# Attention and a two-layer MLP on one core: the last pair of chunks as seven block products, one more staging slot, four sums moved to VectorE, and ranks in the static order

## The chip, the cores and the metric

The kernel runs on one core of one Trainium2 chip. The metric is the device time of one execution in microseconds (us), as the median of several executions of each kernel. Lines named L... are lines of the kernel before.

## The reference

For 4 batches, 12 heads, 448 tokens and a head size of 64, all in float32:

```python
scores = scale * q @ k.T                    # per head, 448 x 448
scores = cap * tanh(scores / cap)           # cap = 30
attn = exp(scores) / sum(exp(scores))
x = attn @ v                                # heads joined: 4 x 448 x 768
u = x + (x.T @ U @ V).T                     # U: 448 x 32, V: 32 x 448
out = u + relu(u @ w_ch1) @ w_ch2           # 768 -> 3072 -> 768
```

## The kernel before

The program is written as a list of tasks. Each task names the engine (or engines) it may run on, a duration in a planner's units, what it reads and writes, and a priority; a smaller number goes first. A list scheduler (`Plan.simulate`) runs the tasks on a model of the five engines, and the order in which it starts them is the order in which each engine's instructions are then written down. Buffers are given out in that run as well: a buffer waits until a slot of one of its pools is free. The chip sees only the fixed order of each engine and the waits between them. SyncE (SP) issues the loads and the stores, GpSimd (POOL) issues the DMAs that add onto a tile or that rearrange, ScalarE (ACT) keeps weights in DRAM.

Attention comes first. The 24 pairs of heads are taken four at a time (`four`). For each block of keys TensorE makes scores (L459), ScalarE takes tanh (L464) and exp (L474), TensorE multiplies by v (L488 for the last 64 keys of two pairs, L500 for three blocks of 128 keys), and VectorE adds up the exponentials of the three blocks (`add`, L506, into tile es). `normalize` then handles two pairs: TensorE sums es over the partitions by a matmul with ones (L539, tile misc), the sums go to sr, POOL spreads them over the partitions (r<-sr), VectorE takes reciprocals, POOL writes them to DRAM and broadcasts them back (rb<-rd, L563), and VectorE multiplies (`norm`, L568, u<-u,rb). For the last 64 keys there are two ways. Pairs 0 to 11 (p < ALONE = 12) add them into es on VectorE by a third L506 on 64 partitions; pairs 12 to 23 leave them to four more matmuls on TensorE per `normalize` (L542, `rest`). `mixin` makes the products with U and V (L590 transposes, L606, L626) and adds onto u (L630).

The MLP follows in two halves of two batches each (n = 0 and 1), 12 chunks of 256 hidden rows in each half. The up products of a chunk are seven block products of nine matmuls instead of eight (`up_seven`, L829); the operands x are made by `operands` and the weights ws by `strassen_weights` (L657, L664). Weights of the first half are loaded from the inputs (wr<-in_w, 768 KB) and kept in DRAM in converted form, the second half loads the kept ones. In the first half each chunk is multiplied down by plain products (`down`, L894, six matmuls a group). In the second half the chunks of a pair are multiplied down together as seven block products (`down_seven`, L1021, operands in `down_operands`), with 126 matmuls for a pair. QUADS = 5 says that five of the six pairs go this way; the last two chunks go by `down`, with 144 matmuls.

A result that has to be added onto u takes one of two ways: VectorE adds it (L899, L1039), or ScalarE copies it to a staging tile st and POOL issues a DMA that adds it (a pour: L907, L1044). The tiles cx of `up_seven` in the first half and st share one set of slots of 128 x 448, five in all: two in pool xe and three that lie in space that attention leaves. A slot is free when its pour has landed. Last, `last_sums` (L1050) adds the three blocks of tile vs (shown as g) onto both halves of the last batch on VectorE.

Of the kernel before, what the change touches and what calls it, by code (L numbers as in the profile page):

```python
# [19 lines left out]
DM = H * D  # L20
# [16 lines left out]
ALONE = 12  # L37
FILL, FIRST = 18, 5
# [3 lines left out]
class Pool:  # L42
# [19 lines left out]
    def part(self, b, opened):  # L62
        if self.whole is None:
            p, g = self.within
            self.whole = opened(p).tile([128, NP, S], self.parts[0], tag=g, name=self.name, bufs=1)
        return self.parts[1][self.at(b)][b.slot](self.whole)
# [194 lines left out]
class Build(Plan):  # L261
    def __init__(self, tc, qk, v, u, vv, w1, w2, cap, ident, out):
# [8 lines left out]
        self.wp = Pool("wp", {"wa": 2, "w1": 3, "g": 3, "ws": 4, "ta": 3}, shared={"gp": "g"})  # L271
        self.wx = Pool("wx", {"x": 1})
        self.wq = Pool("wq", {"wr": 2}, shared={"wl": "wr"})
        self.pre = Pool("pre", {"th": 3, "qk": 2, "es": 2})
        self.xe = Pool("xe", {"x": 3, "cx": 2}, after=(self.pre,), shared={"st": "cx"})
# [4 lines left out]
        self.gx = [Pool("gx", {"g": 1}, after=(self.an, self.aq), within=w, shared={"gp": "g"}) for w in ((self.aq, "xx"), (self.an, "rb"))]  # L280
        self.ap = Pool("ap", {"qk": 3, "vn": 2, "th": 4, "es": 2}, side="right")
        self.late = Pool("late", {"x": 4, "ws": 3, "wa": 1}, after=(self.ap,), side="right")
# [109 lines left out]
    def attention(self):  # L392
# [8 lines left out]
        self.gz = Pool("gz", {"gp": 3}, after=(self.g0,), within=(self.ua, "u0"), parts=(F32R, {"gp": thirds}))  # L401
# [15 lines left out]
    def four(self, p):  # L417
# [26 lines left out]
        for g in range(7):  # L444
# [3 lines left out]
            for j in range(2):  # L448
# [22 lines left out]
                self.task({"ACT": 920}, tanh, r=[(ps, 0)], w=[(th, j)], prio=prio)  # L471
# [7 lines left out]
        for h in range(2):  # L479
# [12 lines left out]
            for i, o in enumerate(os):  # L492
# [31 lines left out]
    def normalize(self, p):  # L524
# [5 lines left out]
        rest = p >= ALONE  # L530
# [105 lines left out]
    def operands(self, bs, order, prio):  # L636
# [3 lines left out]
        pools = (self.wx, self.xe, self.late) if bs[0] == 0 else (self.xe, self.late)  # L640
# [71 lines left out]
    def weights(self, f, first, begin, prio):  # L712
        tag, pool = ("w1", self.wp) if first or f // CF != 2 * QUADS else ("wl", self.wq)
        w = self.buf(tag, [128, 2, DM], F32R, pool)
# [19 lines left out]
    def moe(self):  # L734


        self.kept, rest = {}, []
        order, pend = 10, None
        for n, bs in enumerate(((0, 1), (2, 3))):
# [6 lines left out]
            for c in range(NCH):  # L746
# [3 lines left out]
                four = n and c < 2 * QUADS  # L750
# [12 lines left out]
                if four and c % 2 == 0:  # L763
                    pools = (self.gw, self.g1)
                    if c < 2 * QUADS - 2:
                        pools = (self.g0, *pools) if c % 4 else (*pools, self.g0)
                    last = {(b, j): self.buf("gq", [128, 2, S], F32, *pools) for b, j in ((1, 1), (0, 0), (0, 1), (1, 0))}
                for k, _ in zip(turns, self.up_seven(bs, fs, xs, ws, gs, order, last if four else None, c % 2)):
# [5 lines left out]
                if four:  # L774
                    if c % 2:
                        gq = last
                elif n:
                    rest.append((bs, fs, w1, gs, False))
                    if c == NCH - 1:
                        for _, fs, w1, _, _ in rest:  # L780
                            w1.update((f, self.weights(f, False, 0, 3)) for f in fs)
                else:
                    pend = bs, fs, w1, gs, True
                order += 20
        self.last_sums(bs, vs)
        for x in rest:
            for _ in self.down(order, *x):
                pass
            order += 20

    def relu(self, b, f, src, key, gs):
        nc = self.nc
        tag, pools = ("g", (self.wp, *self.gx)) if b < 2 else ("gp", (self.gz, self.wp, *self.gx))
        g = gs[b, f] = self.buf(tag, [128, 2, S], F32R, *pools)
# [8 lines left out]
    def up_seven(self, bs, fs, xs, ws, gs, order, gq, k):  # L803
# [5 lines left out]
        for x in ("c22", "c11", "c12"):  # L809
            cx[x] = gq[blocks[x]] if gq else self.buf("cx", [128, S], F32, self.xe, *self.rows)  # L810
# [70 lines left out]
    def down(self, order, bs, fs, w1, g, pour):  # L881
        nc = self.nc
        for i, b in enumerate(bs):
            u = self.u_bufs[b]
            for d in range(ND):
# [17 lines left out]
                if pour and k % 2:  # L903
                    st = self.buf("st", [128, S], F32, self.xe, *self.rows)
# [9 lines left out]
                if fs[-1] == NF - 1:  # L914
                    self.task({"SP": 350}, lambda b=b, d=d, u=u: nc.sync.dma_start(
                        out=self.out[b, 128 * d:128 * d + 128], in_=u.t[:, d]), r=[(u, d)], lat=2500, prio=-200)
# [3 lines left out]
    def down_operands(self, m, gq, prio):  # L920
# [9 lines left out]
        H = DM // 2  # L930

# [27 lines left out]
        def w_slot(p):  # L959
            w = wo[p] = self.buf("w1", [128, 2, 2, H], F32R, self.wp)  # L960
            return [((lambda i=i: w.t[:, i]), [(w, i, k) for k in range(2)]) for i in range(2)]

        def g_slots(p):
            h, l = go[p] = [self.buf("g", [128, 2, S], F32R, self.wp, *self.gx) for _ in range(2)]
# [4 lines left out]
        for p in PORDER:  # L969
# [30 lines left out]
    def down_seven(self, order, bs, m, gq, vs):  # L1000
        nc = self.nc
        wo, go = self.down_operands(m, gq, 3)
# [4 lines left out]
        at = iter([o + 3 * i + 1 + e for h, o in enumerate((order, order + 20)) for i in range(7) for e in range(1 + (i + h) % 2)])  # L1007
        bank = {}
        for n, (p, d) in enumerate((p, d) for p in PORDER for d in range(3)):
# [24 lines left out]
            yield  # L1034

    def onto(self, ps, out, key, pour):
# [5 lines left out]
        st = self.buf("st", [128, S], F32, self.xe, *self.rows)  # L1042
# [4 lines left out]
    def last_sums(self, bs, vs):  # L1047
        for u, d0 in ((self.u_bufs[bs[1]], 0), (self.u_bufs[bs[1]], 3)):
            for d in range(3):
                self.task({"DVE": 620}, lambda u=u, d=d, d0=d0: self.nc.vector.tensor_tensor(  # L1050
# [57 lines left out]
```

## Time and profile before

| what | us |
|---|---|
| median of 3 executions | 870.61 |
| lowest and highest | 863.97, 870.93 |
| profiled execution, its own time | 869.8 |
| span of the profiled execution | 867.9 |

The span runs from the first to the last instruction of the program; 1.9 us of the execution lie around it. TensorE is the engine PE; its weight loads are the row PEld. Granted clock 1.00 is 2.4 GHz, and a stretch with a smaller mean holds time at 1.2 GHz. "idle before" is the time that an engine stood before an instruction, with what ended it.

### The profile page before, as it was taken

To read this page: it belongs to the slowest core of one execution; us is meant where nothing else is said; L and a number is where in the kernel's file an instruction comes from. 1 tells how busy PE (TensorE), PEld (TensorE's weight loads), DVE (VectorE), ACT (ScalarE), POOL (GpSimd) and SP (SyncE) were. 2 spreads that over 40 slices of the span, in tenths; PEclk is the share of its full clock that TensorE was granted. 3 is DMA by queue.
4 is the path that set the end of the run, shared out by engine and by line. 5 is a ranking of instruction groups with operands and counts; after the bars stand their busy time and mean duration, and the time that the engine had idled before them with its cause. 6 is when DMAs were issued, how large, how long until landed. Compare 5 with 4: busy or idle time off the path is not lost.

```text
span 867.9 us, 11802 instructions
## 1 busy us (share of the span) xinstructions
PE 851.3 (98%) x4314; PEld 677.4 (78%) x4314; DVE 678.5 (78%) x1131; ACT 518.2 (60%) x771; POOL 134.2 (15%) x174
## 2 busy tenths in 40 slices
PE   9999998999999999998999999999999999999998
PEld 5343442435899999997999999999999999999997
DVE  2798887867987777876777789788888788888864
ACT  7999897987554555535554455455655555555610
POOL 0111111111121111211111111101111111211110
PEclk9999999999999999999999999999999999999999
DMA  6753344422578787897887754914426354452413
GB/s 220 251 166 102 119 140 133 129 65 60 147 212 263 207 248 204 221 244 215 220 249 203 231 161 92 269 40 98 133 43 163 77 137 96 78 164 42 98 33 128
DMA packets 49338, 132.38 MB, mean 153 GB/s; under 512 B 6496, under 2 KB 25344, under 8 KB 49280
## 3 DMA queue, kind: packets, MB, share of 16 engines
q1 hardware_dynamic: 23024, 79.29, 28.3%
q0 software_dynamic: 19344, 33.46, 21.3%
q10 hardware_dynamic: 6912, 18.88, 5.5%
q8 instruction: 34, 0.56, 0.3%
q14 instruction: 24, 0.20, 0.1%
HBM read 79.28 MB, written 24.47 MB: 120 GB/s over the span
## 4 chain that ended last, share of the span: by engine, by line
PE 53%; DVE 0%; issue 0%
PE mm L829 25%; PE mm L1021 15%; PE mm L894 13%; DVE cx L842 0%; DVE u L899 0%; DVE wa L308 0%
## 5 line engine op out<-in xcount | busy, mean ns | idle before, releaser
L829 PE MATMUL mm<-x,ws 128*128 128x448 f32 x1512 | 333.6, 367 | 1.2 <-DVE x L664 1.2
L829 PEld LDWEIGHTS mm<-x,ws 128*128 128x128 f32 x1512 | 283.7, 188 | 27.4 <-DVE x L664 1.5
L894 PE MATMUL mm<-g,w 128*128 128x448 f32 x864 | 188.1, 367 | 2.5 <-ACT st L254 2.0
L894 PEld LDWEIGHTS mm<-g,w 128*128 128x128 f32 x864 | 162.8, 189 | 17.3 <-ACT st L254 2.4
L1021 PE MATMUL mm<-g,w 128*128 128x448 f32 x630 | 139.9, 366 | 0.0
L254 ACT ACTIVATE st<-mm 128x448 f32<-128x448 f32 x121 | 65.9, 545 | 120.1 <-PE mm L894 61.8
L1021 PEld LDWEIGHTS mm<-g,w 128*128 128x128 f32 x630 | 118.2, 188 | 10.6
L907 POOL DMA_DIRECT2D u<-st x72 | 62.9, 873 | 265.1 <-ACT st L254 265.1
L464 ACT ACTIVATE th<-sc,qsc 128x896 f32<-128x896 f32 x84 | 80.5, 1005 | 11.2 <-PE sc L459 7.0
L899 DVE TENSOR_TENSOR u<-u,mm 128x448 f32<-128x448 f32 x96 | 59.4, 620 | 34.1 <-PE mm L894 32.3
L459 PE MATMUL sc<-qk 64*128 64x448 f32 (+1 forms) x384 | 76.8, 567 | 1.2 <-ACT th L464 1.2
L474 ACT ACTIVATE th<-th,capt 128x1792 f32<-128x1792 f32 x42 | 75.3, 1794 | 1.0
L1044 POOL DMA_DIRECT2D u<-st x45 | 38.8, 863 | 218.8 <-ACT st L254 173.8
L500 PE MATMUL o<-th,vn 128*64 128x448 f32 x288 | 59.4, 548 | 0.0
L664 DVE TENSOR_TENSOR ws<-ta,ws 128x384 fp32r<-128x384 f32 x96 | 52.9, 552 | 7.0 <-ACT ws L254 6.6
L308 DVE SCALAR_TENSOR_TENSOR wa<-wa,wr 128x768 int32<-128x768 int32 (+2 forms) x50 | 46.7, 936 | 14.1 <-ACT wa L300 13.2
L459 PEld LDWEIGHTS sc<-qk 64*128 64x128 f32 (+1 forms) x384 | 26.8, 173 | 34.4 <-issue 18.8
L506 DVE TENSOR_TENSOR es<-es,th 128x896 f32<-128x896 f32 (+1 forms) x36 | 39.1, 1087 | 11.6 <-ACT th L474 11.1
L300 ACT ACTIVATE wa<-wr 128x768 f32<-128x768 f32 (+2 forms) x50 | 44.0, 884 | 3.9 <-DMA kept<-wa 1.8
L254 ACT ACTIVATE cx<-mm 128x448 f32<-128x448 f32 x42 | 22.9, 545 | 38.0 <-PE mm L829 24.6
L500 PEld LDWEIGHTS o<-th,vn 128*64 128x64 f32 x288 | 18.5, 136 | 34.5 <-issue 32.4
L1039 DVE TENSOR_TENSOR u<-u,mm 128x448 f32<-128x448 f32 x45 | 27.9, 620 | 22.3 <-PE mm L1021 20.9
(116 smaller groups left out, 984.4 us busy)
## 6 DMA issues: line engine op xcount, KB each, us to landing
wr<-in_w SPq DMA_DIRECT2D x48, 768.0 KB, 5.8
u<-st POOLq DMA_DIRECT2D x117, 224.0 KB, 4.1
kept<-wa ACTq DMA_DIRECT2D x48, 384.0 KB, 5.9
qk<-in_qk SPq DMA_DIRECT2D x24, 448.0 KB, 4.1
wa<-kept SPq DMA_DIRECT2D x28, 384.0 KB, 4.0
wr<-kept SPq DMA_DIRECT2D x20, 384.0 KB, 4.0
vn<-in_v SPq DMA_DIRECT2D x12, 448.0 KB, 3.9
rb<-rd POOLq DMA_DIRECT2D x24, 224.0 KB, 3.9
```

The lines of the kernel that those rows point to most:

```text
L254: e.activation(out=out, in_=in_, func=func)
L308: nc.vector.scalar_tensor_tensor(out=a_t().bitcast(I32), in0=a_t().bitcast(I32), scalar=3, in1=raw_t()[:, 0::2], op0=ALU.logical_shift_lef ...
L459: nc.tensor.matmul(ps.t[out, a, :S], qks[c].t[hd, 1, 128 * t:min(S, 128 * t + 128)], qks[c].t[hd, 0], start=True, stop=True)
L464: nc.scalar.activation(out=th.t[:, j], in_=ps.t[:, :, :S], func=AF.Tanh, scale=self.qsc)
L474: nc.scalar.activation(out=th.t, in_=th.t, func=AF.Exp, scale=self.capt)
L500: nc.tensor.matmul(o.t[64 * a:64 * a + 64, :S], vn.t[:, 3 * i + t, a], th.t[:, j, a], start=False, stop=t == 2)
L664: e.tensor_tensor(out=lo, in0=src(), in1=hi.bitcast(F32), op=ALU.subtract)
L829: nc.tensor.matmul(ps.t[:, :S], ws[p].t[:, wi, sl], xs[p].t[:, xi, d], start=fresh and n == 0, stop=n == 8, skip_group_check=not fresh)
L894: nc.tensor.matmul(ps.t[:, :S], w1[f].t[:, wi, sl], g[b, f].t[:, gi], start=f == fs[0] and i == 0, stop=f == fs[-1] and i == 2)
L899: nc.vector.tensor_tensor(out=u.t[:, d], in0=u.t[:, d], in1=ps.t[:, :S], op=ALU.add)
L907: nc.gpsimd.dma_start(out=u.t[:, d], in_=st.t, accum_op=ALU.add)
L1021: nc.tensor.matmul(ps.t[:, :S], w[:, wi, k, sl], g[gi][:, k], start=fresh and n == 0, stop=n == 5, skip_group_check=not fresh)
```

## The change

- The sixth pair of chunks of the second half also goes through `down_seven` (QUADS is gone). It takes its products in another order, PLAST = 3, 1, 6, 5, 2, 7, 4, and four more places for operands (pools `fin`) in space that the x tiles leave. Of its results the first five products pour (product 5 excepted, which VectorE adds straight onto both halves of the last batch), the last two are added by VectorE. The stores of the second half stand behind it.
- `last_sums` becomes two POOL DMAs that add three blocks (672 KB) each.
- One more slot for cx and st, in pool wp; the scratch of POOL's DMA descriptors goes from 4096 to 2048 bytes a partition.
- SUMS = 20 takes the place of ALONE for the sums: pairs 12 to 19 add their last 64 keys on VectorE, and only pairs 20 to 23 keep the matmuls.
- `rank` adds a fixed number to the priorities of attention's stages and of the preparation for the MLP, and multiplies some planned DMA delays. EARLY, the order in which the first half's operands are made, is another.

```diff
-QUADS = 5
+PAIRS = NCH // 2
 PORDER = 2, 3, 1, 6, 5, 7, 4
+PLAST = 3, 1, 6, 5, 2, 7, 4
-EARLY = 5, 6, 3, 2, 7, 1, 4
+EARLY = 5, 6, 2, 3, 4, 1, 7
 ALONE = 12
+SUMS = 20
+RANK = (
...
+    ("four.add", 47),
...
+    ("normalize.sums", -175),
...
+    ("convert", 108),
...
+)
-        self.wp = Pool("wp", {"wa": 2, "w1": 3, "g": 3, "ws": 4, "ta": 3}, shared={"gp": "g"})
+        self.wp = Pool("wp", {"wa": 2, "w1": 3, "g": 3, "ws": 4, "ta": 3, "cx": 1}, shared={"st": "cx"})
...
+        self.fin = [Pool("fin", {"w1": 1, "g": 1}, after=(p,), within=(p, "x"), parts=(F32R, {
+            "w1": [w1], "g": [lambda t: t[:, 4:6]]})) for p in (self.xa, self.xa, self.xl, self.xl)]
...
-                if p < ALONE:
+                if p < SUMS:
...
-        rest = p >= ALONE
+        rest = p >= SUMS
...
         self.last_sums(bs, vs)
-        for x in rest:
-            for _ in self.down(order, *x):
-                pass
-            order += 20
+        for _ in self.down_seven(order + 10, bs, PAIRS - 1, gq, vs):
+            pass
...
+            elif p == 5 and final:
+                for x in (d, 3 + d):
+                    self.onto(ps, *block(u1, x), False)
             else:
-                self.onto(ps, out, key, n % 2)
+                self.onto(ps, out, key, n % 2 if not final else n < 15)
...
     def last_sums(self, bs, vs):
...
+        u = self.u_bufs[bs[1]]
+        for d0 in (0, 3):
+            self.task({"POOL": 1000}, lambda d0=d0: self.nc.gpsimd.dma_start(
+                out=u.t[:, d0:d0 + 3], in_=vs.t, accum_op=ALU.add), r=[(vs, d) for d in range(3)],
+                w=[(u, d0 + d) for d in range(3)], lat=9000, prio=-200)
+
+    def rank(self):
+        for t in self.tasks:
...
+            if -150 < t.prio < 0:
+                t.prio += next((r for x, r in RANK if stage.startswith(x)), 0)
+            if t.lat:
+                t.lat *= next((k for x, k in SLOW.items() if stage.startswith(x)), 1)
```

The ranks and the larger SUMS move instructions on every engine. Three places matter below.

SP, the loads in the middle and at the end of attention (in_qk and in_v are attention's, in_w the MLP's weights of 768 KB). Before:

```order
L433 DMA qk<-in_qk 128x896 x2
L686 DMA wr<-in_w 128x1536
L439 DMA vn<-in_v 128x896
L433 DMA qk<-in_qk 128x896 x2
L686 DMA wr<-in_w 128x1536
L439 DMA vn<-in_v 128x896
L433 DMA qk<-in_qk 128x896 x2
L439 DMA vn<-in_v 128x896
L433 DMA qk<-in_qk 128x896 x2
L439 DMA vn<-in_v 128x896
L433 DMA qk<-in_qk 128x896
L686 DMA wr<-in_w 128x1536 x42
```

Now:

```order
L467 DMA qk<-in_qk 128x896 x2
L720 DMA wr<-in_w 128x1536
L473 DMA vn<-in_v 128x896
L467 DMA qk<-in_qk 128x896 x2
L473 DMA vn<-in_v 128x896
L467 DMA qk<-in_qk 128x896 x2
L473 DMA vn<-in_v 128x896
L467 DMA qk<-in_qk 128x896 x2
L473 DMA vn<-in_v 128x896
L467 DMA qk<-in_qk 128x896
L720 DMA wr<-in_w 128x1536 x43
```

One of the two single weight loads of this place has moved behind the last of attention's loads.

VectorE at the adds of pairs 12 and 13 (es<-es,th is an add of exponentials, 64x896 the new third one; u<-u,rb is the multiplication that waits for the broadcast). Before:

```order
L256 CAST ys<-misc 128x256
L506 TENSOR_TENSOR es<-es,th 128x896
L617 TENSOR_TENSOR ys<-misc,ys 32x256
L256 COPY u_956<-o 128x448
L506 TENSOR_TENSOR es<-th 128x896
L630 TENSOR_TENSOR u_578<-u_578,misc 128x448 x2
L568 TENSOR_TENSOR u_956<-u_956,rb 128x896
L506 TENSOR_TENSOR es<-es,th 128x896
```

Now:

```order
L540 TENSOR_TENSOR es<-es,th 64x896
L540 TENSOR_TENSOR es<-th 128x896
L635 TENSOR_TENSOR xx<-misc,xx 112x512
L540 TENSOR_TENSOR es<-es,th 128x896
L698 TENSOR_TENSOR x<-u_197,x 128x448
L286 COPY u_935<-o 128x448
L286 CAST ys<-misc 128x256
L540 TENSOR_TENSOR es<-es,th 64x896
L651 TENSOR_TENSOR ys<-misc,ys 32x256
L698 TENSOR_TENSOR x<-u_197,x 128x448
L602 TENSOR_TENSOR u_935<-u_935,rb 128x896
```

The adds stood behind the multiplication that waits for a broadcast, and now stand ahead of it; two more adds on 64 partitions have come in.

TensorE behind the last up products (x9) of the second half, where the products of the last two chunks begin. Before:

```order
L829 MATMUL mm<-x,ws 128x448 x9
L894 MATMUL mm<-gz,wl 128x448 x6
L1021 MATMUL mm<-g,w_7329 128x448 x6
L829 MATMUL mm<-x,ws 128x448 x9
L1021 MATMUL mm<-g,w_7329 128x448 x12
L894 MATMUL mm<-gz,wl 128x448 x30
L894 MATMUL mm<-gp,wl 128x448 x3
```

Now:

```order
L851 MATMUL mm<-x,ws 128x448 x9
L1049 MATMUL mm<-g,w_7319 128x448 x12
L851 MATMUL mm<-x,ws 128x448 x9
L1049 MATMUL mm<-g,w_7319 128x448 x6
L1049 MATMUL mm<-g,w_7402 128x448 x18
L1049 MATMUL mm<-g,w_7440 128x448
L1049 MATMUL mm<-fin,w_7440 128x448
```

Chunk 10 had its first plain group among the last up products; now six matmuls of the fifth pair and then the sixth pair's first product (w_7402) follow the last up product.

## Rows read from the trace of the kernel before

**Rows 1.** The page: busy time of each engine; the chain that ended last, by line.
```profile
PE 851.3 (98%) x4314; PEld 677.4 (78%) x4314; DVE 678.5 (78%) x1131; ACT 518.2 (60%) x771; POOL 134.2 (15%) x174
...
PE mm L829 25%; PE mm L1021 15%; PE mm L894 13%; DVE cx L842 0%; DVE u L899 0%; DVE wa L308 0%
```

**Rows 2.** Windows: length, busy us of PE, PEld, DVE, ACT, POOL; clock; DMA share, GB/s.
```profile
150.00:200.00 50.00, 50.00 (x302) 20.48 (x300) 35.46 (x53) 43.97 (x45) 8.08 (x14) 1.00 0.31 85
...
650.00:750.00 100.00, 100.00 (x490) 91.67 (x489) 83.50 (x139) 56.56 (x97) 17.32 (x20) 1.00 0.47 109
```

**Rows 3.** Timeline of PE (start, us): sums without and with L542, and what follows.
```profile
90.17 0.96 PE L539 MATMUL misc<-es,ones 128*32 128x448 f32 x8
91.06 0.65 PE L590 MATMUL misc<-ident,u 128*112 128x128 f32 x4
...
158.98 0.96 PE L539 MATMUL misc<-es,ones 128*32 128x448 f32 x8
...
160.62 0.65 PE L590 MATMUL misc<-ident,u 128*112 128x128 f32 x4
```

**Rows 4.** Timeline of PE at the sums of pairs 12 and 13.
```profile
138.20 0.94 PE L539 MATMUL misc<-es,ones 128*32 128x448 f32 x2
141.82 0.96 PE L539 MATMUL misc<-es,ones 128*32 128x448 f32 x3 [2.68 <-DVE es L506]
...
144.96 0.69 PE L590 MATMUL misc<-ident,u 128*112 128x128 f32 x4
```

**Rows 5.** Timeline of DVE at that place.
```profile
139.67 1.09 DVE L568 TENSOR_TENSOR u<-u,rb 128x896 f32<-128x896 f32 x1 [4.44 <-DMA rb<-rd]
140.68 1.08 DVE L506 TENSOR_TENSOR es<-es,th 128x896 f32<-128x896 f32 x1
```

**Rows 6.** Timeline of POOL: the broadcast that DVE waits for in rows 5.
```profile
130.25 1.05 POOL L563 DMA_DIRECT2D rb<-rd  x2 [1.74 <-DMA rd<-r]
```

**Rows 7.** Timeline of SP's queue at that time.
```profile
130.28 0.33 SPq L686 DMA_DIRECT2D wr<-in_w  x1
```

**Rows 8.** Windows around both stalls (columns as in rows 2).
```profile
134.00:136.00 2.00, 2.00 (x13) 0.70 (x12) 1.23 (x3) 1.97 (x2) 0.00 (x0) 1.00 1.06 327
...
404.00:412.00 8.00, 5.70 (x21) 4.52 (x20) 6.72 (x12) 4.75 (x9) 0.93 (x2) 0.79 0.58 192
412.00:420.00 8.00, 8.00 (x41) 7.36 (x40) 5.28 (x11) 4.48 (x8) 1.69 (x2) 1.00 0.73 193
```

**Rows 9.** Timeline of ACT before 404 us.
```profile
403.83 0.54 ACT L254 ACTIVATE cx<-mm 128x448 f32<-128x448 f32 x1 [4.80 <-DMA u<-st]
```

**Rows 10.** Timeline of PE: waits in the MLP.
```profile
213.91 1.89 PE L829 MATMUL mm<-x,ws 128*128 128x448 f32 x8 [1.19 <-DVE x L664]
...
406.44 1.49 PE L894 MATMUL mm<-g,w 128*128 128x448 f32 x6 [1.97 <-ACT st L254]
```

**Rows 11.** Tile st: issues (ns min/median/max), who waited (us, times), landing.
```profile
L907 POOL DMA_DIRECT2D u<-st x72: 844/867/1034, 229.7 to 552.1; - x72
...
  ACT st L254: 15.8, 7
...
DMA to landing us min/median/max: 3.1/4.0/9.8
```

**Rows 12.** Lines of DVE by form: count, busy us, mean ns of one.
```profile
L506 DVE TENSOR_TENSOR es<-es,th 64x896 f32<-64x896 f32 x12 | 13.0, 1079 | 0.3
...
L947 DVE TENSOR_TENSOR g<-gw,g 128x896 fp32r<-128x896 f32 x17 | 18.5, 1088 | 1.6 <-PE mm L1021 1.0 <-ACT g L254 0.5
```

**Rows 13.** Lines of ACT by form.
```profile
L254 ACT ACTIVATE st<-mm 128x448 f32<-128x448 f32 x49 | 26.6, 544 | 36.5 <-PE mm L1021 27.1 <-issue 6.2 <-ACT ws L254 1.4
L254 ACT ACTIVATE g<-gw 128x896 fp32r<-128x896 f32 x17 | 16.1, 947 | 1.5 <-DVE gw L940 1.3
```

**Rows 14.** The page: DMA issues, KB each, us to landing.
```profile
wr<-in_w SPq DMA_DIRECT2D x48, 768.0 KB, 5.8
```

**Rows 15.** Timeline of DVE: the last add.
```profile
864.46 0.62 DVE L899 TENSOR_TENSOR u<-u,mm 128x448 f32<-128x448 f32 x1 [0.61 <-PE mm L894]
```

More of the change, by code (lines that the diff above doesn't have):

```diff
@@ L29 @@
 NCH = NF // CF
-QUADS = 5
+PAIRS = NCH // 2
 PORDER = 2, 3, 1, 6, 5, 7, 4
+PLAST = 3, 1, 6, 5, 2, 7, 4
 ORDER = 5, 1, 2, 6, 3, 7, 4
-EARLY = 5, 6, 3, 2, 7, 1, 4
+EARLY = 5, 6, 2, 3, 4, 1, 7
 ALONE = 12
+SUMS = 20
+RANK = (
+    ("four.scores/PE/sc", 3),
+    ("four.scores/PE/q", -7),
+    ("four.tanh", 12),
+    ("four.exp", 2),
+    ("four.rest", 52),
+    ("four.full", 85),
+    ("four.add", 47),
+    ("four.<lambda>/ACT+DVE", -12),
+    ("normalize.sums", -175),
+    ("normalize.<lambda>/ACT+DVE", 14),
+    ("normalize.spread", -76),
+    ("normalize.<lambda>/DVE", 32),
+    ("normalize.norm", -7),
+    ("mixin.transposes", -31),
+    ("mixin.high", 19),
+    ("mixin.low", -34),
+    ("mixin.products", -38),
+    ("mixin.<lambda>/ACT+DVE", 27),
+    ("mixin.y_low", -35),
+    ("mixin.mix", -14),
+    ("mixin.add", -20),
+    ("convert", 108),
+    ("part", 62),
+    ("weights", 6),
+    ("operands", 56),
+)
+SLOW = {"four.load": 1.24, "normalize.spread": 1.00, "normalize.put": 1.25, "normalize.get": 0.72, "block.load": 1.02, "four.tanh": 1.99}
 FILL, FIRST = 18, 5
@@ L470, in four @@
                     self.task({"PE": 750}, scores, r=[*r, (pss[1], "next")], w=[(ps, 0)], prio=-300, mode="q" if t == 3 else "sc")
[L471 removed]
+                self.task({"ACT": 960}, tanh, r=[(ps, 0)], w=[(th, j)], prio=prio)
             def exp(th=th):
@@ L762, in moe @@
                     order += 12
[L763 to L766, printed above, removed]
+                if n and c % 2 == 0:
+                    pools = (self.g0, self.gw, self.g1) if c % 4 else (self.gw, self.g1, self.g0)
                     last = {(b, j): self.buf("gq", [128, 2, S], F32, *pools) for b, j in ((1, 1), (0, 0), (0, 1), (1, 0))}
-                for k, _ in zip(turns, self.up_seven(bs, fs, xs, ws, gs, order, last if four else None, c % 2)):
+                for k, _ in zip(turns, self.up_seven(bs, fs, xs, ws, gs, order, last if n else None, c % 2)):
                     for _ in range(k):
@@ L809, in up_seven @@
         for x in ("c22", "c11", "c12"):
-            cx[x] = gq[blocks[x]] if gq else self.buf("cx", [128, S], F32, self.xe, *self.rows)
+            cx[x] = gq[blocks[x]] if gq else self.buf("cx", [128, S], F32, self.wp, self.xe, *self.rows)
         def to(x):
@@ L879, in up_seven, with down @@
         yield
-    def down(self, order, bs, fs, w1, g, pour):
+    def down(self, order, bs, fs, w1, g):
         nc = self.nc
@@ L902, in down @@
                     w=[(ps, 0)], prio=at, mode="mm")
-                if pour and k % 2:
-                    st = self.buf("st", [128, S], F32, self.xe, *self.rows)
+                if k % 2:
+                    st = self.buf("st", [128, S], F32, self.wp, self.xe, *self.rows)
                     def onto(u=u, d=d, st=st):
@@ L930, in down_operands @@
         H = DM // 2
+        more = self.fin if m == PAIRS - 1 else ()
         def wpart(i, j):
@@ L1031, in down_seven, with store @@
                     prio=-200)
+            elif p == 5 and final:
+                for x in (d, 3 + d):
+                    self.onto(ps, *block(u1, x), False)
             else:
-                self.onto(ps, out, key, n % 2)
+                self.onto(ps, out, key, n % 2 if not final else n < 15)
             yield
+        if final:
+            for i in range(2):
+                for d in range(ND):
+                    self.store(bs[i], d)
+    def store(self, b, d):
+        u = self.u_bufs[b]
+        self.task({"SP": 350}, lambda: self.nc.sync.dma_start(out=self.out[b, 128 * d:128 * d + 128], in_=u.t[:, d]),
+            r=[(u, d)], lat=2500, prio=-200)
     def onto(self, ps, out, key, pour):
```

71 lines of the change are left out of this document (36 added, 35 removed).

## The prediction

> **What bounds the kernel now.** I read the page first, then the windows by stage, then TensorE's timeline wherever a window was not full, and from each gap back to what ended it. The reader should see in [rows 1] that TensorE is busy for 851.3 of 867.9 us and that the chain that ended last runs through its three MLP products alone, while VectorE has 22% and ScalarE 40% of the span free. In the windows [rows 2] full stretches hold 490 matmuls in 100 us, one per 0.204 us; even attention's later part (150 to 200 us) is full. So this kernel gets shorter in two ways only: fewer matmuls, or fewer of the places where TensorE stands.
>
> Two such places are large. At 138 us the sums of pairs 12 and 13 start, and TensorE then stands 2.68 us for an add of VectorE; the block ends at 144.96, so it took 6.76 us [rows 4], where the same block later takes 160.62 - 158.98 = 1.64 us [rows 3]. That is 5.1 us lost, more than the idle time, because the later part of the block ran at a lower clock. The cause is upstream: the add stood in VectorE's queue behind the multiplication u<-u,rb, which waited 4.44 us for the broadcast rb [rows 5]. POOL issued that broadcast at 130.25 [rows 6], it was there by 139.67, 9.4 us later, and SP had issued a weight load of 768 KB 0.03 us after it [rows 7]; the DMA share was 1.06 meanwhile [rows 8].
>
> At 404 us ScalarE stands 4.80 us before it copies cx, until a pour landed [rows 9]: cx and st share five slots, and the next one was still being read. TensorE then stands 1.97 us for ScalarE's st [rows 10]. The window 404 to 412 holds 21 matmuls at a mean clock of 0.79, the next one 41 at 1.00 [rows 8]: 20 x 0.204 = 4.1 us lost.
>
> **The change part by part.** The sum goes against the profiled execution's own time, 869.8 us, which is 0.8 below the median of 870.61, so I carry it over unchanged.
>
> *Sixth pair.* 144 plain matmuls become 126. 18 x 0.204 = 3.7 us less, all on TensorE's path, provided the operands of each product are there in time. I walked the static order by hand from T, the end of the last up product. Six matmuls (1.2 us) of the fifth pair come first; the seven products then start at T + 1.2, 4.9, 8.6, 12.2, 15.9, 19.6 and 23.3, and end at T + 26.9. The first needs c22: its product ends 27 matmuls before T + 1.2, thus at T - 4.3; then an add (0.62), a relu (0.58), the high part (0.95) and the low part (1.09 [rows 12, 13]) make 3.2 us and some waits: ready near T - 0.6. The tightest is the third. Its low part stands on VectorE behind four adds and subtractions on 128x896 and several half-size ones, which by the same durations end at about T + 8.7, against the start at T + 8.6. I take 0.2 us of wait there. Bounds: 0, and 3.7 (the stage gives back all it gains).
>
> *The end.* VectorE's last add follows the last product as it did before (0.62 us [rows 15]), and one store follows that. The twelve pours of this stage are POOL's: the last copies to st come at T + 21.3, issue 0.87, landing 4.0 [rows 11], thus T + 26.2, just before the last add. That is no cost, but with a margin of about 1 us; by the slowest landing of 9.8 it is 5 us.
>
> *last_sums by DMA.* Six adds of VectorE (6 x 0.62) leave a stage where they lay beside TensorE: nothing gained. The two DMAs of 672 KB have no row of their kind. Bounds: 3.1 us (the fastest pour, a third of the size) and 29.4 us (three of the slowest) [rows 11]; I take 5.8, the load of 768 KB [rows 14], the row nearest in size. The second is issued near T - 0.2, behind it POOL's queue goes on, and the first reader of its blocks is VectorE's add of the fourth product, at T + 14.9. So anything up to 14 us costs nothing; at 29.4 VectorE would stand 15 us with the last product's operands queued behind. The Trainium skill, "DMA: Bandwidth & Descriptors", section "Anatomy of one DMA — SWDGE (gpsimd) path", fits such a DMA as 2.0 us plus its bytes at 436 GB/s. By that I estimate 3.6 us for 672 KB, and 2.5 us for the pours. The trace's pours take 4.0 at the median instead, so the fit is too low here; by either the term stays 0.
>
> *Sums of pairs 12 to 19.* Four `normalize` steps lose the L542 matmuls. Sums with them take 1.64 us, without them 91.06 - 90.17 = 0.89 us [rows 3]: 0.75 x 4 = 3.0 us off TensorE. VectorE gets 8 adds of 1.08 us on 64 partitions [rows 12]: 8.6 us over the 80 us or so of these pairs, where it has 14.5 of every 50 us free [rows 2]. Hidden, unless an add is the last thing that the sums wait for: that is the second rival.
>
> *Ranks.* In the new order the adds of pairs 12 and 13 stand ahead of the multiplication that waits for a broadcast, and the weight load that collided with the broadcast stands behind attention's last load. Both causes of the stall at 138 us are gone: 5.1 us. A late broadcast would now hold up `mixin`, not the sums. The moved load has a price: VectorE's conversion of that block now falls in the first chunk of the MLP, where TensorE already waits for VectorE (1.19 us once [rows 10]). The other small waits of the reordered stages have no row of after; I bound them by -3 us (they vanish) and +5.1 us (one more stall as at 138 us) and take +0.6, about half of the 1.19 us wait.
>
> *Sixth slot.* A sixth slot puts one more use between a slot's pour and its next writer. A chunk of the first half uses 9 slots (3 cx, 6 st) in some 28 us, one per 3.1 us, so the wait of 4.80 us becomes 1.7 us. TensorE's wait of 1.97 us came out of those 4.80, so a wait 3.1 us shorter leaves none: 4.1 us gone. ScalarE's other waits for pours (7 for st, 15.8 us [rows 11]) shrink too, but cost TensorE nothing today. The halved descriptor scratch: POOL has at most a few pours under way, each of 128 rows, and no row shows an issue over 1.03 us [rows 11]; I take 0.
>
> Sum: 869.8 - 3.7 + 0.2 - 3.0 - 5.1 + 0.6 - 4.1 = 854.7 us.
>
> **The rivals.**
>
> *The slot is not the cure (12%).* Under a DMA share of 1.0 the pours may land 9.8 us late with six slots too, and ScalarE still stand long enough to starve TensorE once. For: the stall needs only one pour like the slowest. Against: one use is 3.1 us and TensorE's share of the wait was 1.97. Time: 854.7 + 4.1 = 858.8.
>
> *The sums wait for the third adds (8%).* VectorE's queue runs in order. If each of the four changed sums stands behind an add that is late and the clock falls as in [rows 4], each costs 5.1 us: the one stall stays and three come, 854.7 + 5.1 + 15.3 = 875.1, slower than before. It decides from 4 stalls on: with three the gain of 15.1 us against 869.8 is just eaten. For: VectorE gets 8.6 us more in this stage. Against: 29% of it is free.
>
> *The end waits for pours (10%).* The last three pours land as the slowest did: T + 21.3 + 0.9 + 9.8 = T + 32.0 instead of T + 27.5, and the store comes after that: 854.7 + 4.5 = 859.2. Against it speaks the low DMA load of the end.
>
> *VectorE blocks POOL (3%).* The issues of the twelve pours could each stretch by one VectorE instruction of 1.09 us to 1.96 us. From T + 3.3 on, 12 x 1.96 = 23.5 us put the last issue's end at T + 26.8 and its landing at T + 30.8, against T + 27.5: 854.7 + 3.3 = 858.0. Against: with VectorE busy 83.5% [rows 2] no pour's issue needed more than 1.03 us. The Trainium skill, "SBUF — State Buffer", section "SBUF: two separate sides", says that POOL cannot write its DMA descriptors while VectorE holds the shared port in its fast modes. By that rule moving adds from VectorE to POOL pours in a busy stage is a loss; the trace does not bear it out.
>
> *Cheaper work, same end (7%).* The removed sums lay where TensorE would have waited anyway, for ScalarE's tanh and exp (busy 44 of 50 us in [rows 2]): 854.7 + 3.0 = 857.7.
>
> **How the numbers follow.** The forecast itself has 60%, with its own range of 850 to 860. Predicted time: 854.7 us. The range for all is 847 (the small waits go as well, and the tight third operand costs nothing: 854.7 - 0.6 - 3 - 0.2 = 850.9, and the start of the MLP with it) to 866 (two of the rivals' costs together, 4.1 + 4.5, and a little more). Faster by over 1% means below about 861.9; 1% is also about what a measurement tells from no change. The forecast's own 60% lie below it nearly whole (58), of the rivals without the second about two thirds (21 of 32): faster 79%. Within 1%: what is left of these and a third of the second rival, 15%. Slower by over 1%: 6%.
>
> **What would show it.** TensorE's windows should hold 490 matmuls per 100 us everywhere from 20 us on; what was L542 should be left with a third of its matmuls; the sums of pairs 12 to 19 should follow each other to the next line in 0.89 us; no ACT wait for a pour should be followed by a TensorE wait; the seven last products should run from T + 1.2 to T + 26.9 without a gap, and VectorE's last add, not a pour, should be ahead of the last store. The prediction is wrong if TensorE stands over 2 us at a sum, if a window behind 205 us has a clock below 1.00, or if the products of the sixth pair show idle time above 1 us.

## The result, and the profile after

The changed kernel takes 855.07 us (median of 4 executions, 852.21 to 856.73) beside 868.89 for the kernel before in the same rounds: ratio 0.9855, interval 0.9825 to 0.9886. Five more executions, later, gave 857.08 us (855.69 to 858.43) beside 868.41: 0.9868 [0.9847, 0.9890]. Forecast were 854.7 us and a range of 847 to 866. The total came out right; two of its terms, the two stalls that were read from one execution, did not, as the experiments show.

The page of the changed kernel: busy time of each engine, the chain that ended last, and the pours among the DMA issues.

```profile
PE 840.4 (99%) x4264; PEld 671.4 (79%) x4264; DVE 691.0 (81%) x1144; ACT 527.6 (62%) x789; POOL 146.1 (17%) x188
...
PE mm L851 21%; PE mm L1049 18%; PE mm L916 4%; DVE cx L864 0%; DVE u L1079 0%; DVE wa L343 0%
...
u<-st POOLq DMA_DIRECT2D x129, 224.0 KB, 4.1
```

Against [rows 1], VectorE is busy for 12.5 us more, POOL for 11.9 and ScalarE for 9.4, TensorE for 10.9 less: work has moved from the engine that bounds the kernel to others that have room. The windows of the changed kernel (length, busy us of PE, PEld, DVE, ACT, POOL, clock, DMA share, GB/s), to be held against [rows 2, 8]:

```profile
100.00:150.00 50.00, 49.26 (x284) 19.53 (x282) 45.16 (x66) 48.08 (x50) 7.04 (x12) 1.00 0.44 136
150.00:200.00 50.00, 49.96 (x295) 20.68 (x291) 45.10 (x70) 40.31 (x42) 7.11 (x12) 1.00 0.33 100
400.00:450.00 50.00, 50.00 (x248) 46.25 (x247) 39.03 (x69) 25.70 (x45) 9.49 (x11) 1.00 0.83 239
...
820.00:848.00 28.00, 27.66 (x136) 25.19 (x135) 22.28 (x31) 14.79 (x26) 11.99 (x14) 1.00 0.97 204
```

In this execution the stretches around 140 and 404 us are all but full and run at a clock of 1.00; another one of the same kernel (after_2 below) had a stretch at 0.50. Attention's sums and the places where the two stalls were, on TensorE's timeline (start, us, and in brackets the idle time before and what ended it), to be held against [rows 3, 4, 10]:

```profile
138.26 0.96 PE L573 MATMUL misc<-es,ones 128*32 128x448 f32 x8 [0.47 <-DVE u L664]
139.16 0.65 PE L624 MATMUL misc<-ident,u 128*112 128x128 f32 x4
...
212.94 2.09 PE L851 MATMUL mm<-x,ws 128*128 128x448 f32 x9 [0.81 <-ACT cx L284]
...
477.49 1.49 PE L916 MATMUL mm<-g,w 128*128 128x448 f32 x6 [0.23 <-ACT st L284]
```

The sums take 139.16 - 138.26 = 0.90 us as forecast, after a wait of 0.47 us instead of 2.68. The largest wait behind a pour is 0.23 us instead of 1.97.

The end, in the chain of waits (start, us, piece):

```profile
818.98 1.83 PE mm L851 x9
820.80 26.88 PE mm L1049 x132
847.68 0.02 issue
847.70 0.62 DVE u L1079
```

From the last up product on, 132 matmuls in 26.88 us, 0.2036 each, with no gap; an add of VectorE, not a pour, stands ahead of the last store.

### The profile page after: what moved, and what is told of

It reads as the page before. It is cut to its first block, busy times and chain, and to the rows that moved or that the text cites. A ratio compares the mean times of both kernels' runs of the same rounds, so it can differ in the third digit from the quotient of the medians.

```text
span 851.8 us, 11737 instructions
## 1 busy us (share of the span) xinstructions
PE 840.4 (99%) x4264; PEld 671.4 (79%) x4264; DVE 691.0 (81%) x1144; ACT 527.6 (62%) x789; POOL 146.1 (17%) x188
## 5 line engine op out<-in xcount | busy, mean ns | idle before, releaser
L916 PE MATMUL mm<-g,w 128*128 128x448 f32 x864 | 187.0, 366 | 0.6 <-DVE cx L864 0.3
L916 PEld LDWEIGHTS mm<-g,w 128*128 128x128 f32 x864 | 162.0, 188 | 15.0 <-ACT st L284 0.9
L1049 PE MATMUL mm<-g,w 128*128 128x448 f32 x696 | 154.9, 366 | 0.0
L284 ACT ACTIVATE st<-mm 128x448 f32<-128x448 f32 x133 | 72.4, 544 | 113.7 <-PE mm L916 55.2
L1049 PEld LDWEIGHTS mm<-g,w 128*128 128x128 f32 x696 | 130.6, 188 | 11.8
L929 POOL DMA_DIRECT2D u<-st x72 | 62.5, 868 | 268.9 <-ACT st L284 263.8
L1084 POOL DMA_DIRECT2D u<-st x57 | 49.4, 866 | 224.1 <-ACT st L284 161.4
L498 ACT ACTIVATE th<-sc,qsc 128x896 f32<-128x896 f32 x84 | 80.3, 1005 | 11.9 <-PE sc L493 11.7
L921 DVE TENSOR_TENSOR u<-u,mm 128x448 f32<-128x448 f32 x72 | 44.5, 618 | 21.6 <-PE mm L916 19.9
L1079 DVE TENSOR_TENSOR u<-u,mm 128x448 f32<-128x448 f32 x57 | 35.0, 619 | 23.3 <-PE mm L1049 21.7
L540 DVE TENSOR_TENSOR es<-es,th 128x896 f32<-128x896 f32 (+1 forms) x44 | 47.5, 1082 | 6.0 <-ACT th L508 5.5
L284 ACT ACTIVATE ws<-ta 128x384 fp32r<-128x384 f32 x64 | 32.9, 519 | 15.2 <-PE mm L851 8.9
```

What stands on the lines that cost most here:

```text
L284: e.activation(out=out, in_=in_, func=func)
L498: nc.scalar.activation(out=th.t[:, j], in_=ps.t[:, :, :S], func=AF.Tanh, scale=self.qsc)
L540: e.tensor_tensor(out=out(), in0=in0(), in1=in1(), op=ALU.add)
L916: nc.tensor.matmul(ps.t[:, :S], w1[f].t[:, wi, sl], g[b, f].t[:, gi], start=f == fs[0] and i == 0, stop=f == fs[-1] and i == 2)
L929: nc.gpsimd.dma_start(out=u.t[:, d], in_=st.t, accum_op=ALU.add)
L1049: nc.tensor.matmul(ps.t[:, :S], w[:, wi, k, sl], g[gi][:, k], start=fresh and n == 0, stop=n == 5, skip_group_check=not fresh)
```

## The experiments

Each kernel is the one before or the changed one with the edit named. The profiled execution is one of each kernel's; medians and intervals are over all its executions.

| kernel | what it is | median us | ratio to before, 95% |
|---|---|---|---|
| m_norm | before, one VectorE instruction a row later | 865.42 | 0.9960 [0.9943, 0.9978] |
| m_load | before, one weight load later | 866.70 | 0.9989 [0.9966, 1.0012] |
| a_slot | before + sixth slot | 866.88 | 0.9995 [0.9972, 1.0018] |
| a_sums | before + SUMS = 20 | 869.30 | 1.0023 [0.9998, 1.0047] |
| a_seven | before + sixth pair in seven products | 865.20 | 0.9955 [0.9932, 0.9977] |
| a_rank | before + ranks | 872.67 | 1.0049 [1.0026, 1.0071] |
| b_both | before + ranks + SUMS = 20 | 859.63 | 0.9898 [0.9878, 0.9918] |
| u_slot | changed - sixth slot | 857.77 | 0.9887 [0.9855, 0.9919] |
| u_sums | changed, SUMS = 12 | 881.66 | 1.0144 [1.0107, 1.0182] |
| x_keep | changed, its order, L542's work put back | 861.33 | 0.9911 [0.9891, 0.9931] |
| t_mix | changed, two groups of products ahead of the first transposes | 858.53 | 0.9880 [0.9859, 0.9901] |
| after_2 | changed, once more | 857.08 | 0.9868 [0.9847, 0.9890] |

The first four ran beside a before of 867.74 us, a_seven, a_rank, u_slot and u_sums beside 868.51, the others beside 868.41. Single executions of the kernel before spread over some 9 us (863.97 to 873.01 in 31), so the stalls of one profiled execution needn't come in another.

**m_norm and m_load: the stall at 138 us.**

```diff
# m_norm
-            self.task({"DVE": 1090}, norm, r=[(rb, 0)], w=[(u, q), (u, q + 1)], prio=prio, lock=True)
+            self.task({"DVE": 1090}, norm, r=[(rb, 0)], w=[(u, q), (u, q + 1)], prio=prio + 2 * (p == 13), lock=True)
# m_load: the sixth in_w load stands behind vn and two qk loads on SP, its first conversion later on VectorE
```

> The kernel before with one multiplication by the broadcast (u<-u,rb of pairs 12 and 13) placed one row later on VectorE, behind the add of exponentials that the stalled sums wait for; nothing else moves. Theory (order): the sums no longer wait for a broadcast, so 5.1 us go (3 to 5.5), although the broadcast itself still lands some 9 us after its issue. Rival (collision): the late broadcast is what costs, the wait only moves to the transposes behind it, and the time changes by 0 to -2 us.

> The kernel before with one weight load of 768 KB on SP moved behind three of attention's loads (and its first conversion step moved behind on VectorE); the order of the adds and the multiplication stays. Theory (collision): the broadcast issued with that load lands in about 4 us instead of 9.4, the multiplication hardly waits, and 5.1 us go (3 to 5.5). Rival: the broadcast is slow for another reason, attention's own loads, and the time changes by less than 1.5 us.

With the multiplication one row later (add and multiplication change places) the sums on TensorE wait for nothing; with the load moved, they don't either, but the transposes of the next block do. TensorE of m_norm, then of m_load:

```profile
140.04 0.96 PE L539 MATMUL misc<-es,ones 128*32 128x448 f32 x8
140.82 0.94 PE L542 MATMUL misc<-th,ones 128*32 128x448 f32 x8
...
143.49 1.02 PE L459 MATMUL sc<-qk 64*128 64x448 f32 x4 [0.20 <-ACT th L464]
145.31 0.98 PE L488 MATMUL o<-th,vn 64*64 64x448 f32 x8 [0.80 <-ACT th L474]
```
```profile
158.93 0.65 PE L590 MATMUL misc<-ident,u 128*112 128x128 f32 x4 [1.91 <-DVE u L568]
```

So the stall needs both, the place in VectorE's order and the late broadcast: either edit takes it away. Only the place pays. Over many executions it is worth 2.3 us by the medians (867.74 - 865.42) and 3.5 by the ratio, not the 5.1 us read from one. In m_load this broadcast is used 5.2 us after its issue instead of 9.4, but the moved load now goes out at 149.56, beside the next broadcast (149.29), which is used 8.5 us after its issue, at 157.78.

Two profiles show why 5.1 us was too much. In m_norm's, TensorE waits 1.0 us for ScalarE soon after (0.20 and 0.80, lines above). And in a_slot's, whose order is that of the kernel before up to 232 us, the same stall is 2.07 us and the block takes 143.32 - 138.67 = 4.65 us, 3.0 more than 1.64, at a clock of 1.00; in the profile of the kernel before the clock was 0.72 from 140 to 146 us. TensorE of a_slot:

```profile
138.67 0.94 PE L539 MATMUL misc<-es,ones 128*32 128x448 f32 x2
141.68 0.58 PE L539 MATMUL misc<-es,ones 128*32 128x448 f32 x3 [2.07 <-DVE es L506]
...
143.32 0.65 PE L590 MATMUL misc<-ident,u 128*112 128x128 f32 x4
```

**a_slot and u_slot: the sixth slot.**

```diff
-        self.wp = Pool("wp", {"wa": 2, "w1": 3, "g": 3, "ws": 4, "ta": 3}, shared={"gp": "g"})
+        self.wp = Pool("wp", {"wa": 2, "w1": 3, "g": 3, "ws": 4, "ta": 3, "cx": 1}, shared={"gp": "g", "st": "cx"})
...
```

> The kernel before with the sixth slot for cx and st alone (and the smaller descriptor scratch that makes room). Theory: ScalarE's wait of 4.8 us for a pour becomes 1.7 us or less, TensorE's wait of 1.97 us at 404 us goes, and the time falls by 4.1 us (2.5 to 4.5). Rival: the slow pour is as late for six slots, TensorE still stands and drops its clock once: 0 us.

> The changed kernel with five staging slots instead of six. The prediction's sizing: the stall at 404 us comes back, 4.1 us, so about 859 us beside 855.1. My theory by now, since the sixth slot alone changed nothing on the kernel before (0.9995): 0 to 1 us, 855 to 856, with ScalarE's waits for pours longer and TensorE's waits behind them under 1 us.

ScalarE of a_slot, with six slots, and TensorE behind it:

```profile
402.18 0.54 ACT L254 ACTIVATE cx<-mm 128x448 f32<-128x448 f32 x1 [4.08 <-DMA u<-st]
402.62 1.68 ACT L300 ACTIVATE wa<-wr 128x768 f32<-128x768 f32 x2
404.19 0.53 ACT L254 ACTIVATE st<-mm 128x448 f32<-128x448 f32 x1
...
404.78 1.50 PE L894 MATMUL mm<-g,w 128*128 128x448 f32 x6 [1.18 <-ACT st L254]
```

The wait that was 4.80 us [rows 9] is 4.08 with one slot more, not 1.7. Even the 0.7 us between them are not the slot's: with five slots and the old order of this stage the same wait is 3.90 us in m_norm and 3.41 in m_load, and TensorE behind it waits 1.07 and 0.48 us, against 1.18 in a_slot. The lines between show why TensorE feels it: behind cx two conversions of weights (1.68 us) stand ahead of the st that frees TensorE's bank. ScalarE and TensorE of m_norm, then the window of the stall in m_norm and in a_slot:

```profile
401.28 0.55 ACT L254 ACTIVATE cx<-mm 128x448 f32<-128x448 f32 x1 [3.90 <-DMA u<-st]
...
403.88 1.50 PE L894 MATMUL mm<-g,w 128*128 128x448 f32 x6 [1.07 <-ACT st L254]
...
404.00:412.00 8.00, 7.68 (x37) 6.77 (x38) 7.40 (x15) 3.21 (x7) 1.74 (x2) 1.00 0.91 292
...
404.00:412.00 8.00, 6.90 (x33) 6.07 (x34) 7.40 (x15) 3.94 (x9) 1.74 (x2) 1.00 0.78 257
```

The clock stays at 1.00 in both; the 0.79 of [rows 8], which made 4.1 us out of a wait of 1.97, is in the profile of the kernel before alone. b_both has five slots and the new order, and ScalarE there still waits 3.48 us:

```profile
478.89 0.55 ACT L283 ACTIVATE cx<-mm 128x448 f32<-128x448 f32 x1 [3.48 <-DMA u<-st]
...
481.51 1.49 PE L923 MATMUL mm<-g,w 128*128 128x448 f32 x6 [0.67 <-ACT st L283]
```

TensorE waits 0.67 us and its clock stays; in u_slot, five slots too, no wait of TensorE behind a pour is left, and with six slots it is 0.23 (the changed kernel) and 0.4 (after_2). So these waits of TensorE are shorter in the new order, with either number of slots. ScalarE's own waits for pours come to 20.3 us in u_slot, 21.6 in the changed kernel and 17.6 in after_2: no profile shows a gain of the slot. In time the slot is between nothing (a_slot) and 2.7 us (u_slot against 855.07; 0.7 against 857.08), and the intervals don't decide between these. u_slot's order differs from the changed kernel's in a few rows only, at ScalarE near 216 us and in the last pair, so it is the better test of the two; a_slot's differs from that of the kernel before in many rows from 232 us on.

**a_seven: the last pair alone.** The diff is the change's own without SUMS, ranks, EARLY, slot and scratch.

> The kernel before with the sixth pair of chunks as seven block products and nothing else (five staging slots, rest sums of pairs 12 to 19 on TensorE, the old order, the old descriptor scratch). My theory: 18 matmuls fewer at 0.204 us on TensorE's path, 3.7 us less 0.2, so about 864 us beside 867.7 for before, and the products of the last pair without a gap. Rival 'the end gives it back' (the first operands, or the last pours, are late): no change, with idle time of TensorE or a later last store in the last 30 us.

3.3 us by the medians, 3.9 by the ratio; forecast 3.5. The planner laid another order for attention here too, so the times alone do not single out the last pair. The traces do. What follows the last up product on TensorE, in the kernel before and in the changed one:

```profile
833.80 2.40 PE L1021 MATMUL mm<-g,w 128*128 128x448 f32 x11
```
```profile
820.64 1.59 PE L1049 MATMUL mm<-g,w 128*128 128x448 f32 x7
```

The last add starts 864.46 - 833.80 = 30.7 us later before [rows 15], and 847.70 - 820.64 = 27.1 us later now: 3.6 us less. From the end of the last up product to that of the last product TensorE takes 30.5 us in each of the seven profiles without the seven products here and 26.9 to 27.0 in each of the seven with them. The last store gives a little back: it ends 851.8 - 848.32 = 3.5 us after the last add, where it was 867.9 - 865.08 = 2.8 before.

**a_rank, a_sums and b_both: ranks and sums.** Diffs: `self.rank()` ahead of `simulate` with RANK, SLOW and EARLY of the change; `SUMS = 20`; both.

> The kernel before with the last keys of pairs 12 to 19 added on VectorE alone, without ranks. Theory: 16 matmuls leave TensorE's path, 4 x 0.75 = 3.0 us less (2 to 4) with the two large stalls left where they are. Rival: the sums wait for the third adds, each such wait costs up to 5.1 us, and the time is the same or longer (0 to +15 us).

> The kernel before with the new order alone (ranks, latency factors, the new order of the products). My theory, after the multiplication moved by one row gave 2.3 us: the ranks take away the stall of the sums near 140 us and most small waits before 240 us, 3 to 6 us, so 862 to 865 us beside 867.7; the wait near 404 us stays in the executions that have it. Rival 'ranks only pay with the cheaper sums': no change (866.5 to 869), with waits at the sums or transposes of pairs 12 to 19.

> The kernel before with ranks and with the rest sums of pairs 12 to 19 on VectorE, without the sixth slot and without the seven products. Theory 'the two only pay together': the ranks alone were 4.2 us slower and the sums alone no faster, but the changed kernel gains some 13 us of which the seven products have 3 to 4 and the slot about 3, so about 861 to 862 us beside 868.5. Rival 'each adds its own': 869 to 873 us.

The sums alone gain nothing, the ranks alone cost 4.2 us, both together gain 8.8 (868.41 - 859.63). The theory for a_sums (3.0 us less) and that for a_rank (3 to 6 less) both failed. By the ratios 0.9898 x 0.9955 = 0.9853, the whole change: with the seven products nothing is left over for the slot, though each of the three kernels has an order of its own. a_sums and a_rank show a wait that the prediction had not named. TensorE and VectorE of a_sums, then of a_rank:

```profile
189.72 0.96 PE L540 MATMUL misc<-es,ones 128*32 128x448 f32 x8 [2.12 <-DVE u L631]
...
187.92 1.09 DVE L569 TENSOR_TENSOR u<-u,rb 128x896 f32<-128x896 f32 x1 [5.00 <-DMA rb<-rd]
189.04 1.15 DVE L631 TENSOR_TENSOR u<-u,misc 128x448 f32<-128x448 f32 x2
```
```profile
176.02 0.96 PE L567 MATMUL misc<-es,ones 128*32 128x448 f32 x8 [1.91 <-DVE u L658]
...
174.22 1.09 DVE L596 TENSOR_TENSOR u<-u,rb 128x896 f32<-128x896 f32 x1 [3.41 <-DMA rb<-rd]
175.35 1.15 DVE L658 TENSOR_TENSOR u<-u,misc 128x448 f32<-128x448 f32 x2
```

The sums read es, which has been there for a while. They are released by mixin's add u<-u,misc, which neither writes es nor reads it: it reads the misc tile that holds the bank which the sums are to write (the kernel has two banks for misc). That add stands behind the multiplication that waits for its broadcast.

The bank isn't the largest loss of the two kernels. Between 200 and 250 us, where attention ends beside the first chunk of the MLP, TensorE gets through 219 matmuls in a_sums and 223 in a_rank, against 246 in the kernel before and 245 in b_both. Window of a_sums (its profiled execution, 874.11 us, is the slowest of its ten), window of a_rank, and the longest wait of TensorE in the latter, for an operand cx, behind which nine matmuls take 3.41 us instead of 2.09:

```profile
200.00:250.00 50.00, 43.21 (x219) 35.04 (x216) 39.07 (x71) 23.43 (x45) 5.00 (x7) 0.97 0.44 133
...
200.00:250.00 50.00, 43.59 (x223) 35.85 (x223) 37.42 (x66) 24.51 (x47) 6.47 (x9) 0.97 0.42 122
...
226.79 3.41 PE L857 MATMUL mm<-x,ws 128*128 128x448 f32 x9 [1.88 <-DVE cx L870]
```

**u_sums and x_keep: is it the sums' work, or the order?** u_sums lets the planner lay a new order with the heavier sums; x_keep keeps the changed kernel's order and only puts the matmuls back. Beside 16 matmuls of the shape of L542 more (32 in the trace), x_keep's engines have the same instructions in the same order; its sums count es twice.

```diff
# u_sums
-SUMS = 20
+SUMS = 12
# x_keep, in sums() of the changed kernel
...
-            for i in range(4 if rest else 0):
+            for i in range(4 if p >= ALONE else 0):
...
-self.ones[:, 1 + i % 2], rth.t[:, rj, i // 2], start=False, stop=True)
+self.ones[:, 1 + i % 2], e[i % 2].t[:, i // 2], start=False, stop=True)
```

> The changed kernel with the rest sums of pairs 12 to 19 back on TensorE. My theory: 4 x 0.75 = 3.0 us come back, about 858 us, since in the ranked order nothing waits at these sums. Rival (the cheaper sums alone gave nothing on the kernel before, 1.0023): no change, 854 to 856, because the time taken off TensorE is lost in waits.

> The changed kernel in its own order, instruction for instruction, with 16 more matmuls of the shape of L542 at the sums of pairs 12 to 19 (they read es a second time, so the sums are other numbers). Theory 'the price is 0.75 us a sum, the 26 us of u_sums came from another order': 3.0 us more than the changed kernel, about 858 us. Rival 'heavy sums cost more than their matmuls in this order': 865 us or more.

x_keep is 861.33 - 857.08 = 4.25 us slower than after_2 in the same rounds, which agrees with 4 x 0.75 = 3.0 within the intervals. u_sums is 26.6 us slower than the changed kernel, so most of that is order (expected were 3.0). One place of it, TensorE and VectorE of u_sums:

```profile
549.93 7.39 PE L916 MATMUL mm<-g,w 128*128 128x448 f32 x22 [12.98 <-ACT w L284]
...
545.99 1.15 DVE L698 TENSOR_TENSOR x<-u,x 128x448 fp32r<-128x448 f32 x2
...
547.65 0.96 DVE L343 SCALAR_TENSOR_TENSOR wa<-wa,wr 128x768 int32<-128x768 int32 x1
```

400 us after the sums the planner has put the conversion of the first half's last down weights behind the whole run of the second half's x operands on VectorE, and TensorE stands 12.98 us. So "one part alone" measures another order here, and not the part: that holds for a_sums, a_rank and a_seven too. x_keep's profiled execution, the slowest of its seven (865.51 us), also shows the bank at work in the changed kernel's own order:

```profile
142.70 1.55 PE L573 MATMUL misc<-es,ones 128*32 128x448 f32 x8 [2.91 <-DVE u L664]
...
140.90 1.09 DVE L602 TENSOR_TENSOR u<-u,rb 128x896 f32<-128x896 f32 x1 [2.89 <-DMA rb<-rd]
142.03 1.15 DVE L664 TENSOR_TENSOR u<-u,misc 128x448 f32<-128x448 f32 x2
```

The same sums waited 0.47 us in the profile of the changed kernel, 0.93 in u_slot and nothing in after_2: the stall is still there, and shorter or longer by how late the broadcast comes.

**t_mix and after_2: can the largest wait left be had?** Two groups of products, which need nothing from the first transposes, go ahead of them on TensorE.

```diff
         order = self.simulate()
+        name = lambda t: getattr(t.fn, "__qualname__", "")
+        first = next(t for t in order if name(t).endswith("transposes"))
+        at = order.index(first)
+        for n in ("rest", "full"):
+            t = next(t for t in order[at:] if name(t).endswith("four.<locals>." + n))
+            order.remove(t)
+            order.insert(order.index(first), t)
```

> The changed kernel with the first transposes of mixin behind three products of attention on TensorE; nothing else moves. Theory: the wait of 1.69 us at 43.6 us goes and nothing takes its place, 1.5 us less than the changed kernel. Rival: the transposed block is late for its products by as much, no change.

> The changed kernel once more, in the same rounds as x_keep and t_mix: 854 to 856 us. Its profile tells which of its waits come in every execution: by my theory 1.4 to 1.7 us near 43 us and some 0.7 us waits between 204 and 216 us, while a wait at the sums near 140 us stays under 1 us.

t_mix gains nothing: 858.53 us beside 857.08. TensorE of t_mix:

```profile
42.40 0.98 PE L522 MATMUL o<-th,vn 64*64 64x448 f32 x8 [1.09 <-ACT th L508]
...
45.72 0.65 PE L624 MATMUL misc<-ident,u 128*112 128x128 f32 x4
...
52.77 0.51 PE L640 MATMUL misc<-xx,ust 112*128 112x256 f32 x2 [0.78 <-DVE xx L635]
...
60.41 0.96 PE L573 MATMUL misc<-es,ones 128*32 128x448 f32 x8 [1.50 <-DVE u L664]
```

The transposes no longer wait, but exp is next (1.09), and the block that is now late is late at its products (0.78) and at the bank of the next sums (1.50). No kernel here beats the changed one.

after_2 is the changed kernel itself (857.08 us, expected 854 to 856), and its profiled execution took 858.43 us where the first one took 853.6. The sums near 140 us wait for nothing in it, the transposes near 43 us wait 1.85 us (1.69 in the first profile). What it has more is time at the lower clock. Behind that wait its clock is 0.83 over 40 to 50 us, where the first profile has 1.00; and behind a wait of 1.09 us at 207.82 nine matmuls take 3.56 us instead of 2.09. TensorE of after_2, and its window there:

```profile
207.82 1.59 PE L640 MATMUL misc<-xx,ust 112*128 112x256 f32 x4 [1.09 <-ACT xx L284]
209.21 3.56 PE L851 MATMUL mm<-x,ws 128*128 128x448 f32 x9
...
208.00:214.00 6.00, 6.00 (x17) 5.19 (x18) 4.49 (x9) 1.99 (x5) 1.42 (x3) 0.50 0.36 102
```

The prediction had named a window behind 205 us with a clock below 1.00 as a sign that it is wrong. The first profile doesn't show it, this one does.

## Why the prediction was right, and where not

- **Own time as the start.** 869.8 was 0.9 to 1.4 us above what the kernel before gave beside the changed one (868.89, 868.41). The measured gain is 13.8 us by the first medians (12.6 by their ratio) and 11.3 by the second ones; the sum of the terms was 15.1. So the terms were too large by 1 to 4 us together, and the high start hid about 1 of it. That the total lay within 0.4 us of the first median is luck in part; from the second it is 2.4 away.
- **Sixth pair, -3.7 and +0.2: right.** a_seven gives 3.3 to 3.9, the traces 3.6, of which the later last store takes back 0.6. The products followed each other from T + 1.2 on as walked, and ended at T + 26.9. The last copy to st came at T + 19.7 (840.51, forecast T + 21.3) and its pour at T + 20.6 (841.40 on POOL). The two large DMAs landed after 6.1 us each, where 5.8 was taken. One reason was wrong: the end was said to have a low DMA load. Before, the share over 820 to 848 us was 0.23; the change itself fills it to 0.97. The pours landed in time all the same.
- **Sums, -3.0: right in size, wrong as a term of its own.** In a fixed order they are worth 4.25 us, and the interval has room for 3.0 (x_keep). Without the ranks the order that the planner then lays gains nothing (a_sums). The second rival had named sums that wait. Those that wait in a_sums (2.12 and 0.70 us) wait for the bank behind the multiplication, not for the third adds, and more is lost where attention ends beside the MLP.
- **Stall at 138 us, -5.1: the step that failed.** The prediction said that both causes of the stall "are gone". The adds did move ahead of the multiplication, but the sums are still held by the bank that mixin's add reads behind it. And the 5.1 us came from one execution in which the clock fell; a_slot's profile has 3.0 for the same stall, and m_norm, which takes away this stall alone, is worth 2.3 to 3.5. It also named the pairs wrongly: the sums and adds at 138 us are those of pairs 14 and 15, while the multiplication ahead of them is that of pairs 12 and 13.
- **Small waits, +0.6: not borne out.** Ranks and sums together gave 8.8 us (b_both). TensorE's wait at 404 us is smaller there too, so four terms stand against it: 3.0 + 5.1 - 0.6 + 4.1 = 11.6, which is 2.8 too much. With 3.0 for the sums and 2.3 to 3.5 for the first stall, 2.3 to 3.5 us of the 8.8 are left for the small waits and the second stall together; no run parts the two.
- **Sixth slot, -4.1: wrong cause.** "A sixth slot puts one more use between", so the wait was to be 1.7 us: it was 4.08 (a_slot), within the 3.41 to 4.80 us of the kernels with five slots, and taking the slot away from the changed kernel made its waits for pours no longer (u_slot). The size was wrong as well: of the 4.1 us, half was a clock drop that m_norm and m_load, with the same order there, don't have. The first rival had this right, that the slot is not the cure, and was wrong that the stall then stays at its full price: in the new order TensorE waits 0.67 us or less (b_both and u_slot, five slots). Which of its parts did so, the ranks or EARLY, wasn't tried.
- VectorE did not hold up POOL: the pours of the end were issued in 0.85 to 0.89 us with VectorE busy 22.28 of 28 us.

What stays open: how far the ranks alone are slower for the order's own accidents and how far for the heavier sums (a_rank in b_both's order wasn't tried), what the slot is worth below 3 us, and why the clock falls behind a wait in one execution and not behind the same wait in another.

## What to carry to other kernels

Where a planner lays the order, undoing one part gives another order, and a stall hundreds of us away can outweigh the part; hold the order fixed and add or take away the work itself. A stall read from one execution can hold a clock drop that other executions don't have (5.1 and 3.0 us for the same stall), so price it by an edit that removes it alone, or read it from several profiles. When an instruction is moved ahead of a late one, follow the tile that its reader writes as well as those that it reads: the bank may still hang on the late one.

## What the runs showed of the hardware that was not expected

A DMA share of 0.97 over the last 28 us did not delay the pours enough to matter: the DMAs out of st from 800 us on landed after 3.1, 4.6 and 5.4 us (least, median, most), where the whole kernel before has 3.1, 4.0 and 9.8.

A wait of TensorE cost more than its length where the clock fell behind it, and that differed between two executions of one kernel, with the same order on every engine: behind 1.69 us at 43.61 the changed kernel's clock stayed at 1.00 over 40 to 50 us, behind 1.85 at 43.34 in after_2 it was 0.83.

The way of the reciprocals through DRAM, in contrast, decided several us. VectorE waited 2.89 us for a broadcast in the profile of x_keep, and 0.45 us for the same one in that of the changed kernel, whose DMAs are the same in the same order:

```profile
136.47 1.09 DVE L602 TENSOR_TENSOR u<-u,rb 128x896 f32<-128x896 f32 x1 [0.45 <-DMA rb<-rd]
```

The broadcast itself was in use 5.8 us after its issue in the changed kernel and 6.6 in x_keep. More of the difference lies ahead of it, in the write of the reciprocals to DRAM, which POOL awaits before it issues the broadcast. POOL of the changed kernel, then of x_keep:

```profile
130.63 1.05 POOL L597 DMA_DIRECT2D rb<-rd  x2 [1.46 <-DMA rd<-r]
...
134.31 1.06 POOL L597 DMA_DIRECT2D rb<-rd  x2 [3.18 <-DMA rd<-r]
```
